# Retention and channel mix on one core: one group of channel products and its relu pass the state products of the next block and their copy

## The chip, the cores and the metric

The kernel runs on one core of one Trainium2 chip. The metric is the time on the device in microseconds (us), as the median of several executions. The core has five engines with an in-order queue each: TensorE (PE in the profile; PEld is its loading of weights), VectorE (DVE), ScalarE (ACT), GpSimd (POOL) and SyncE (SP). TensorE writes its results to PSUM, which has 8 banks of 128 x 512 float32; the kernel names them 0 to 7.

## The reference

Two layers follow each other. The first is a retention layer over 4 batches, 8 heads, 768 tokens and head width 64: a state of 64 x 64 per head that decays by gamma at each token and takes up k times v.

```python
for t in range(S):
    state = gamma[None, :, None, None] * state + np.einsum('bhd,bhe->bhde', k[:, :, t], v[:, :, t])
    y[:, :, t] = scale * np.einsum('bhd,bhde->bhe', q[:, :, t], state)
```

Its output, with the heads side by side (512 columns), is the x of the second, a channel mix with a shift by one token:

```python
xk = mu_k * x + (1.0 - mu_k) * x_prev
xr = mu_r * x + (1.0 - mu_r) * x_prev
k = np.maximum(xk @ w_k, 0.0)          # 512 -> 1024
v = k * k @ w_v                        # 1024 -> 512
r = 1.0 / (1.0 + np.exp(-(xr @ w_r)))
return (r * v).astype(np.float32)
```

## The kernel before, in words

The 768 tokens of each batch are worked off in three blocks of 256, so there are 12 blocks, 0 to 11; block 3 is the first of batch 1. A block goes through these steps, each with a code:

- `lq`, `lk`, `lv` load q, k and v (`load`, lines 222 to 237), most of them issued by GpSimd. `vs` scales v by powers of gamma into float16 (`scale_v`, L253).
- `Tq`, `Tk` transpose q and k on TensorE (L272, L278), `Eq`, `Ek` copy the result out of PSUM. `S` multiplies k by q (L318, L331, L339), `M` masks it on VectorE (L347, L354).
- `C` makes the state products k times v of the block in two halves, one PSUM bank each (`state`, L384 for blocks 2 to 5: 16 matmuls). `U.n.c` adds half c to the state that is carried along (`summed`, L419); in the first block of a batch there is nothing to add to, and `U.n.0` is a plain copy of the first half into float16 (L407 to 417, by way of `copy`, L241). `G` multiplies the state by the decay of 256 tokens for the next block (`decayed`, L424).
- `I` multiplies the carried state by q (L441), `Y` the masked scores by v (L462, L478), `D` scales the sum into x (L507, L514).
- `dx` and `X` make xk and xr (`differ`, `mixed`). `K.n.g` is a group of the channel products xk @ w_k (`keys`, L582 for a block by itself, L572 for two blocks together): for block 2 a group is two slices of 128 of the 1024 channels, eight matmuls, and the four groups fill one bank each. `Qa.n.g` is the relu of a group, from its bank into a buffer (`relued`, L591), `Qb.n.g` the square of that (`squared`, L599, L603), both on ScalarE.
- `R` and `s` are the gate xr @ w_r and its sigmoid (L612, L618), `V` is the product with w_v (L624, L642), `O` the product with the gate (L630, L649), `st` the store (L637, L657).

What sets the order of the work is a text, `ORDER` (lines 24 to 81), written out by hand: one word for a step, `code.block.part`, then `@` and the PSUM banks or `~` and the engine (v VectorE, a ScalarE, p GpSimd, s SyncE). The loop at lines 755 to 769 walks through it and issues each step; with the manual schedule (line 179) each engine gets its instructions in just this order. Waits follow from what is written and read: a step that writes a bank waits until what was in it has been read.

The change touches line 40 of the text. The words before it that matter are on line 39: `K.2.2@5 Qa.2.2~a K.2.3@4` and `Qa.2.3~a Qb.2.3~a`, `S.3.1@67 M.3.1~v`. Line 40 reads:

```python
S.3.0@01 vs.3~p C.3@23 U.3.0~a Qb.2.2~a K.2.1@4 Qa.2.1~a K.2.0@2 Qa.2.0~a I.3@45 lq.6~p vs.4~v
```

and line 41 begins `C.4@67 U.3.1~v X.2.1.1~v V.0.1.0@3 M.3.0~v V.1.0.0@2 G.3~a U.4.0~v I.4@01`. Here `vs.3` is one of the two scalings that GpSimd does. K.2.1 uses bank 4 as K.2.3 before it; C.3 uses banks 2 and 3; K.2.0 uses bank 2 after C.3. `KR` (line 150) is the set of four buffers between `Qa` and `Qb`, given out in the order in which they come free (lines 588 to 597).

Of the kernel before, what the change touches and what calls it, by code (L numbers as in the profile page):

```python
# [36 lines left out]
Qa.1.2~a s.1.0~a X.0.1.2~v X.0.1.1~v X.0.1.0~v R.0.1@5 s.0.1~a s.1.1~a R.0.0@7 s.0.0~a S.4.1@01  # L37
Qb.1.0~a D.2~v dx.2~v X.2.0.2~v X.2.0.0~v S.4.0@23 Tq.3@4 Eq.3~a X.2.0.1~v wv.1~p X.2.0.3~v Tk.3@7
lq.5~p Ek.3~a K.2.2@5 Qa.2.2~a K.2.3@4 M.4.1~v M.4.0~v Qa.2.3~a Qb.2.3~a lk.6~p S.3.1@67 M.3.1~v
S.3.0@01 vs.3~p C.3@23 U.3.0~a Qb.2.2~a K.2.1@4 Qa.2.1~a K.2.0@2 Qa.2.0~a I.3@45 lq.6~p vs.4~v  # L40
C.4@67 U.3.1~v X.2.1.1~v V.0.1.0@3 M.3.0~v V.1.0.0@2 G.3~a U.4.0~v I.4@01 X.2.1.3~v U.4.1~v J.3
Qb.1.3~a Y.4 Qb.2.0~a lk.5~p X.2.1.2~v X.2.1.0~v Y.3 D.3~v dx.3~v V.0.0.0@7 V.0.1.1 O.0.1~v Tq.5@45
J.4 D.4~v dx.4~v R.2.0@6 Qb.2.1~a V.0.0.1 O.0.0~v X.3.0.1~v Eq.5~a Qb.1.2~a V.1.0.1 X.3.0.2~v
# [756 lines left out]
```

## Time and profile before

| | |
|---|---|
| median of 3 runs | 153.38 us (153.35 to 153.46) |
| the profiled execution | 153.28 us |
| its span, first to last instruction | 151.4 us |
| granted TensorE clock, mean | 1.000 |
| busy: DVE, ACT, POOL | 127.8, 103.6, 55.3 us |
| HBM read, written | 24.16 MB, 6.29 MB |

A row of the time line gives start and duration in us, the engine, the line of the kernel, the operation, the tile written and the tiles read, the shapes, and how many instructions are put together in it. In brackets stands how long the engine was idle before it, and what ended that. Matmuls are pipelined: each lasts longer than the distance from its start to the next one's start, so rows of PE overlap. The chain of waits is followed back from the last instruction to what released each step.

### The profile page before, as it was taken

To read this page: it belongs to the slowest core of one execution; us is meant where nothing else is said; L and a number is where in the kernel's file an instruction comes from. 1 tells how busy PE (TensorE), PEld (TensorE's weight loads), DVE (VectorE), ACT (ScalarE), POOL (GpSimd) and SP (SyncE) were. 2 spreads that over 40 slices of the span, in tenths; PEclk is the share of its full clock that TensorE was granted. 3 is DMA by queue.
4 is the path that set the end of the run, shared out by engine and by line. 5 is a ranking of instruction groups with operands and counts; after the bars stand their busy time and mean duration, and the time that the engine had idled before them with its cause. 6 is when DMAs were issued, how large, how long until landed. Compare 5 with 4: busy or idle time off the path is not lost.

```text
span 151.4 us, 5541 instructions
## 1 busy us (share of the span) xinstructions
PE 143.4 (95%) x2426; PEld 82.8 (55%) x2426; DVE 127.8 (84%) x212; ACT 103.6 (68%) x195; POOL 55.3 (37%) x65
## 2 busy tenths in 40 slices
PE   7878799999999999999999999999999999999991
PEld 3345487757754554547465564548456444655450
DVE  7886999999989999999999999999799999400432
ACT  3565979899844795779567786999604756839420
POOL 7953998577957309996710000000000000000000
PEclk9999999999999999999999999999999999999999
DMA  5999999999999999999999019301000005500433
GB/s 140 219 229 197 207 231 192 168 251 212 196 167 202 233 262 107 256 300 198 231 173 126 7 38 283 105 35 45 0 4 0 4 0 211 205 0 0 148 133 139
DMA packets 45624, 22.16 MB, mean 146 GB/s; under 512 B 37400, under 2 KB 41248, under 8 KB 45600
## 3 DMA queue, kind: packets, MB, share of 16 engines
q0 software_dynamic: 38704, 14.42, 74.5%
q1 hardware_dynamic: 6592, 7.21, 14.3%
q8 instruction: 19, 0.31, 0.8%
q10 hardware_dynamic: 304, 0.18, 0.4%
q14 instruction: 5, 0.04, 0.1%
HBM read 24.16 MB, written 6.29 MB: 201 GB/s over the span
## 4 chain that ended last, share of the span: by engine, by line
PE 73%; DMA 12%; POOL 11%; issue 1%; DVE 0%; POOLq 0%
PE ps L624 27%; PE ps L572 14%; DMA v<-in_v_dram 12%; PE ps L612 12%; PE ps L582 8%; PE ps L278 3%; POOL q L235 3%; POOL k L230 2%; PE ps L441 2%; POOL vs L253 2%; POOL v L230 2%; PE ps L366 1%; PE ps L462 1%; PE ps L642 1%; PE ps L318 1%
## 5 line engine op out<-in xcount | busy, mean ns | idle before, releaser
L624 PE MATMUL ps<-wv,k2s 128*128 128x512 f16 x184 | 44.1, 380 | 0.0
L591 ACT ACTIVATE kr<-ps 128x512 f32<-128x512 f32 x48 | 27.9, 594 | 12.5 <-PE ps L582 6.5
L624 PEld LDWEIGHTS <-k2s 128*128 128x128 f16 x184 | 17.1, 98 | 18.9 <-ACT k2s L603 0.4
L630 DVE SCALAR_TENSOR_TENSOR os<-ps,rs 128x512 f32<-128x512 f32 x23 | 15.6, 684 | 11.9 <-ACT rs L618 9.4
L612 PE MATMUL ps<-wr,xr 128*128 128x512 f16 x96 | 23.5, 379 | 0.0
L582 PE MATMUL ps<-xk,wk 128*128 128x256 f16 x192 | 23.2, 273 | 0.0
L572 PE MATMUL ps<-xk,wk 128*128 128x512 f16 x96 | 23.0, 379 | 0.0
L618 ACT ACTIVATE rs<-ps 128x512 f32<-128x512 f32 x24 | 13.6, 597 | 12.9 <-PE ps L612 12.1
L230 POOL DMA_DIRECT2D k<-in_k_dram x20 | 17.8, 903 | 10.3 <-PE ps L384 6.7
L582 PEld LDWEIGHTS <-wk 128*128 128x128 f16 x192 | 18.1, 98 | 3.7
L241 ACT COPY qT<-ps 128x1024 f16<-128x1024 f16 (+1 forms) x13 | 12.3, 946 | 9.5 <-PE ps L278 7.8
L558 DVE SCALAR_TENSOR_TENSOR xr<-dx,mu,xT 128x256 f16<-128x256 f32 (+1 forms) x32 | 17.9, 577 | 0.1
L230 POOL DMA_DIRECT2D v<-in_v_dram x18 | 16.0, 911 | 3.6 <-DMA wr<-in_moe_w_r_dram 1.9
L558 DVE SCALAR_TENSOR_TENSOR xk<-dx,mu,xT 128x256 f16<-128x256 f32 (+1 forms) x32 | 17.0, 579 | 0.2
L354 DVE TENSOR_TENSOR a<-ps,c_sb 128x1024 f16<-128x1024 f32 (+1 forms) x14 | 14.6, 1066 | 0.9 <-PE ps L339 0.6
L603 ACT ACTIVATE k2s<-kr 128x512 f16<-128x512 f32 x24 | 14.8, 631 | 0.3
L612 PEld LDWEIGHTS <-xr 128*128 128x128 f16 x96 | 9.0, 97 | 10.7 <-issue 0.5
L572 PEld LDWEIGHTS <-wk 128*128 128x128 f16 x96 | 9.1, 98 | 10.5
L599 ACT ACTIVATE k2s<-kr 128x512 f16<-128x512 f32 x24 | 14.5, 627 | 0.3
L241 ACT COPY kT<-ps 128x1024 f16<-128x1024 f16 (+1 forms) x13 | 12.2, 945 | 2.2 <-PE ps L272 1.7
L529 DVE TENSOR_TENSOR dx<-xT 128x1024 f32<-128x1024 f32 x11 | 13.4, 1221 | 0.2
L253 DVE TENSOR_TENSOR vs<-v,csm_sb 128x1024 f16<-128x1024 f32 x10 | 12.2, 1217 | 0.2 <-DMA v<-in_v_dram 0.2
(73 smaller groups left out, 165.6 us busy)
## 6 DMA issues: line engine op xcount, KB each, us to landing
out_dram<-os SPq DMA_DIRECT2D x23, 256.0 KB, 2.4
v<-in_v_dram POOLq DMA_DIRECT2D x18, 256.0 KB, 7.7
q<-in_q_dram POOLq DMA_DIRECT2D x11, 256.0 KB, 8.4
k<-in_k_dram POOLq DMA_DIRECT2D x21, 128.0 KB, 8.8
v<-in_v_dram POOLq DMA_DIRECT2D x2, 512.0 KB, 7.2
wk<-in_moe_w_k_dram POOLq DMA_DIRECT2D x2, 512.0 KB, 10.4
wv<-in_moe_w_v_dram POOLq DMA_DIRECT2D x2, 512.0 KB, 10.4
wr<-in_moe_w_r_dram POOLq DMA_DIRECT2D x1, 512.0 KB, 8.7
```

The costliest lines, as they stand in the source:

```text
L230: e.dma_start(out=dst[:, :, i * D : i * D + D], in_=src[:, i * P : i * P + P].rearrange("h p d -> p h d"),)
L241: e.copy(out=out, in_=in_)
L253: e.tensor_tensor(out=VS(n), in0=V32(n).rearrange("p h (i d) -> p i h d", i=2), in1=gks[:, int(half(n) or wide(n)), :, :, None].to_broadca ...
L354: nc.vector.tensor_tensor(out=a_full(n)[:, i, :, j0:j1], in0=pairs(banks("S", n, i, j0))[:, :, j0:j1], in1=(below if wide(n) else causal[: ...
L558: nc.vector.scalar_tensor_tensor(out=XM[w](k)[:, j, t0:t1], in0=DX(k)[:, j, t0:t1], scalar=mu[:, w * NCO + j : w * NCO + j + 1], in1=x[:, ...
L572: nc.tensor.matmul(banks("K", n, g), lhsT=wk16[:, co, g * P : g * P + P], rhs=XM[0](k)[:, co, :], start=(co == 0), stop=(co == NCO - 1),)
L582: nc.tensor.matmul(pz[:, i, :], lhsT=wk16[:, co, fo * P : fo * P + P], rhs=XM[0](k)[:, co, m * TM + t0 : m * TM + t1], start=(i == 0 and c ...
L591: nc.scalar.activation(out=kr, in_=banks("K", n, g, *u), func=AF.Relu)
L603: nc.scalar.activation(out=K2(n)[:, w * g : w * g + w, t0:t1], in_=kr.rearrange("p a t -> p (a t)").rearrange("p (i t) -> p i t", i=w), fu ...
L612: nc.tensor.matmul(banks("R", n, tb), lhsT=XM[1](k)[:, co, t : t + P], rhs=wr16[:, co, :], start=(co == 0), stop=(co == NCO - 1),)
L624: nc.tensor.matmul(banks("V", n, tb), lhsT=K2(n)[:, fo, tb * P : tb * P + P], rhs=wv16[:, fo, :], start=(fo == 0), stop=(fo == NFO - 1),)
L630: nc.vector.scalar_tensor_tensor(out=OS(2 * n + tb), in0=banks("V", n, tb), scalar=1.0 / (KSC * KSC), in1=RS(2 * n + tb), op0=ALU.mult, op ...
```

## The change

Two words of the order, `K.2.1@4` and `Qa.2.1~a`, move from behind `Qb.2.2~a` to the place in front of `C.3@23`. On TensorE the eight matmuls of K.2.1 then come ahead of the sixteen of C.3; on ScalarE the relu Qa.2.1 comes ahead of the copy U.3.0 and of the square Qb.2.2. All else keeps its place. The text gets a line more, so the lines of the kernel behind it are numbered one higher (K is L583, C.3 is L385).

```diff
-S.3.0@01 vs.3~p C.3@23 U.3.0~a Qb.2.2~a K.2.1@4 Qa.2.1~a K.2.0@2 Qa.2.0~a I.3@45 lq.6~p vs.4~v
+S.3.0@01 vs.3~p K.2.1@4 Qa.2.1~a C.3@23 U.3.0~a
+Qb.2.2~a K.2.0@2 Qa.2.0~a I.3@45 lq.6~p vs.4~v
```

## The prediction

> **What bounds the kernel now.** I read the page's busy times first, then the chain of work that ended last, then what TensorE waits for, and last the time line of each engine around the edited line of the order. The page:
>
> ```profile
> PE 143.4 (95%) x2426; PEld 82.8 (55%) x2426; DVE 127.8 (84%) x212; ACT 103.6 (68%) x195; POOL 55.3 (37%) x65
> PE 73%; DMA 12%; POOL 11%; issue 1%; DVE 0%; POOLq 0%
> ```
>
> TensorE (PE) is busy for 95% of the span, and the chain that ends last is 73% PE. The chain in order of time shows where it goes over to PE (start, duration, what):
>
> ```profile
> 25.54 10.37 DMA v<-in_v_dram
> 35.91 0.07 issue
> 35.98 1.91 POOL vs L253
> 37.89 0.04 issue
> 37.93 0.44 PE ps L384 x16
> 38.37 1.85 PE ps L582 x16
> 40.23 0.23 PE ps L441 x4
> ...
> 148.26 0.02 issue
> ```
>
> So up to 37.93 us the end is set by the load of block 3's v and by GpSimd's scaling of it (`vs.3`). From 37.93 to 148.26 it is PE without a break: C.3 (L384) is the first link, and the 16 matmuls behind it are K.2.1 and K.2.0, eight each. PE's waits from 38 us to the end, and its busy time there, say the same:
>
> ```profile
> PE ps L384 <- POOL vs L253: 0.3, 1, 0.3
> 38.00:148.30 110.30, 110.24 (x1816) 1.00 0.74 126
> ```
>
> There is one wait, the one in front of C.3 (it lies just before 38 us; the group that it released reaches into the window), and 110.24 us busy of 110.30, at a granted clock of 1.00. Whatever the edit adds or saves on PE at about 38 us therefore comes out at the end with almost nothing to soak it up. The time line of PE, then of ScalarE (ACT), around the edit:
>
> ```profile
> 35.12 1.92 PE L582 MATMUL ps<-xk,wk 128*128 128x256 f16 x16
> 36.98 0.62 PE L331 MATMUL ps<-qT,kT 64*128 64x128 f16 x16
> 37.93 0.44 PE L384 MATMUL ps<-vs,k 128*64 128x64 f16 x16 [0.33 <-POOL vs L253]
> 38.30 1.92 PE L582 MATMUL ps<-xk,wk 128*128 128x256 f16 x16
> 40.16 0.30 PE L441 MATMUL ps<-qT,tg 64*64 64x128 f16 x4
> ```
>
> ```profile
> 36.60 1.14 ACT L591 ACTIVATE kr<-ps 128x512 f32<-128x512 f32 x2
> 37.77 0.63 ACT L603 ACTIVATE k2s<-kr 128x512 f16<-128x512 f32 x1
> 38.38 0.37 ACT L241 CAST tg<-ps 128x256 f16<-128x256 f32 x1
> 38.65 0.63 ACT L603 ACTIVATE k2s<-kr 128x512 f16<-128x512 f32 x1
> 39.45 0.60 ACT L591 ACTIVATE kr<-ps 128x512 f32<-128x512 f32 x1 [0.17 <-PE ps L582]
> 40.32 0.60 ACT L591 ACTIVATE kr<-ps 128x512 f32<-128x512 f32 x1 [0.28 <-PE ps L582]
> 40.82 1.05 ACT L424 ACTIVATE tg<-t,csm_sb 128x64 f16<-128x64 f32 x4
> ```
>
> PE in words: K.2.2 and K.2.3, S.3.0, 0.33 us idle, C.3, K.2.1 and K.2.0, I.3. ACT: Qa.2.2 and Qa.2.3, Qb.2.3, U.3.0 (the cast), Qb.2.2, Qa.2.1, Qa.2.0, G.3.
>
> **The change part by part.** No instruction is added or dropped, and the built program has the same rows in another order: on PE the eight matmuls of K.2.1 now stand ahead of the sixteen of C.3; on ACT Qa.2.1 stands ahead of U.3.0 and Qb.2.2. The two moved steps issue no DMA and pass no word of GpSimd's or SP's. So the question is only what each step waits for in its new place. Steps on one PSUM bank must follow each other, and the banks stand in the order: K.2.1 is on bank 4, which K.2.3 used before and Qa.2.3 empties; C.3 is on banks 2 and 3; K.2.0 is on bank 2, which U.3.0 empties of C.3's first half.
>
> *1. K.2.1 goes into the idle time: little of it is left to win.* S.3.0 ends at 36.98 + 0.62 = 37.60. But bank 4 is free only when Qa.2.3 ends, the second of the pair 36.60 + 1.14 = 37.74. For the delay from such an end to PE's start I take 0.05 us: the scaling on GpSimd ends at 35.98 + 1.91 = 37.89 in the chain (37.88 in its own row), and C.3 starts at 37.93; an ACT to PE release shows the same:
>
> ```profile
> 7.08 0.59 ACT L241 COPY qT<-ps 128x512 f16<-128x512 f16 x1
> 7.72 0.42 PE L339 MATMUL ps<-qT,kT 64*64 64x128 f16 x16 [0.69 <-ACT qT L241]
> ```
>
> (7.67 to 7.72.) K.2.1 starts at 37.79. The idle time shrinks from 0.33 to 0.19.
>
> *2. C.3 follows K.2.1.* Sixteen matmuls of this form start 0.11 us apart and one takes 0.27 (0.27 + 15 x 0.11 = 1.92), so eight take 1.04: K.2.1 ends at 38.83. A group of small matmuls behind such a group starts 0.06 us ahead of its end (S.3.0 at 36.98 against 35.12 + 1.92 = 37.04; I.3 at 40.16 against 40.22): C.3 runs from 38.77 to 39.21. Its `vs.3` has then been ready since 37.88, its banks too, so the wait of the old order is gone for good, with 0.9 us to spare.
>
> *3. K.2.0 loses its cover.* In the old order K.2.1 stood between C.3 and K.2.0, for 0.88 us (eight starts 0.11 apart, so that K.2.0 started at 39.18), while U.3.0 took 0.37; the copy cost PE nothing. In the new order nothing stands between, and U.3.0 is late as well, since ACT works in order and Qa.2.1 stands before it. Qa.2.1 starts when K.2.1 has ended; the release from PE to ACT is 0.11 us (K.2.1 of the old order ends at 38.30 + 1.04 = 39.34, Qa.2.1 starts at 39.45). So Qa.2.1 runs from 38.94 to 39.54. U.3.0 overlaps its end by up to 0.10 us, as Qb.2.2 does with U.3.0 (38.38 + 0.37 = 38.75 against 38.65) and G.3 with Qa.2.0 (40.92 against 40.82); it starts at 39.44 and ends at 39.81. C.3's bank 2 is ready at 39.2, so the queue on ACT is what decides, by about 0.2 us. With 0.05 of release K.2.0 starts at 39.86, where the old order has it at 39.18. PE is idle from 39.21 to 39.86, 0.65 us, twice what the old gap was.
>
> The Trainium skill, Perfetto Trace Analysis, section Matmuls (under Optimizing Tensor Performance), speaks against this step: independent matmul groups should rotate through different PSUM banks, so that the evacuation of one lies under the matmuls of the next. K.2.0 directly behind C.3 on bank 2 is the opposite; by that rule a wait of at least the copy is due, and the old trace agrees in so far as the 0.37 us cast lay under K.2.1.
>
> *4. The sum.* K.2.0 then takes what it took, 0.98 us to I.3's start (39.18 to 40.16): I.3 starts at 39.86 + 0.98 = 40.84 against 40.16. That is **+0.68 us**. By parts against the old order, in PE's time up to K.2.0's first matmul: with no wait of either kind K.2.1 would start at 37.53 (0.07 ahead of S.3.0's end, as K.2.1 of the old order stands 0.07 ahead of C.3's end), C.3 0.98 later and K.2.0 another 0.37 later (as 37.93 to 38.30 now), at 38.88, that is 0.30 earlier than now; the wait on Qa.2.3 gives 0.26 of it back (-0.04); the wait on U.3.0 adds 0.72 (+0.68).
>
> *5. Behind it.* Who waits for the moved steps? U.3.1 on VectorE (DVE) needs U.3.0, and U.4.0 needs G.3:
>
> ```profile
> 39.76 0.42 DVE L419 TENSOR_TENSOR t<-ps,tg 128x256 f32<-128x256 f32 x1
> 40.49 1.22 DVE L354 TENSOR_TENSOR a<-ps,c_sb 128x1024 f16<-128x1024 f32 x1
> 41.90 0.42 DVE L419 TENSOR_TENSOR tg<-ps,tg 128x256 f16<-128x256 f32 x1 [0.20 <-ACT tg L424]
> 42.59 0.42 PE L441 MATMUL ps<-qT,tg 64*64 64x128 f16 x12
> ```
>
> U.3.1 starts at 39.86 in place of 39.76, 0.10 late, and DVE has 0.20 idle before U.4.0; free. On ACT Qa.2.0 starts 0.11 behind K.2.0's end (39.86 + 1.04 = 40.90), at 41.01, so G.3 ends 0.69 late; U.4.0 shifts by the same and I.4 (42.59, 0.27 behind U.4.0's end) keeps its slack, since PE shifts too. On GpSimd one load of k must wait until C.3 has read its buffer:
>
> ```profile
> 40.50 0.90 POOL L230 DMA_DIRECT2D k<-in_k_dram  x1
> ```
>
> The first issue comes at 40.50, C.3 ends at 39.21: covered by 1.3 us. I cost all of this at nothing. If the cover failed, each of these is a delay on PE of a few tenths, which is the upper end below.
>
> *6. What could be given back.* After 38 us two groups of gate products (L612) start late on a DVE result, without an idle time that the profile shows:
>
> ```profile
> 30.86 2.76 PE L612 MATMUL ps<-wr,xr 128*128 128x512 f16 x12
> ...
> 64.67 1.89 PE L572 MATMUL ps<-xk,wk 128*128 128x512 f16 x8
> 66.55 1.24 PE L612 MATMUL ps<-wr,xr 128*128 128x512 f16 x5
> ...
> 127.19 2.86 PE L612 MATMUL ps<-wr,xr 128*128 128x512 f16 x12
> ```
>
> ```profile
> 65.81 0.68 DVE L630 SCALAR_TENSOR_TENSOR os<-ps,rs 128x512 f32<-128x512 f32 x1
> ```
>
> Twelve such matmuls take 2.76 us at 30.86 and 2.86 at 127.19, 0.10 more. Twelve in 2.76 and eight in 1.89 mean 0.22 apart, so the one at 66.55 could have come at 64.67 + 8 x 0.2165 = 66.40: 0.15 late (its bank 2 is emptied by the result step of the last row, 65.81 + 0.68 = 66.49, and 0.06 of release). If DVE kept its old times there, PE would lose 0.25 less. But DVE itself is shifted at U.4.0 by G.3, and it works in order; I take 0, with 0.25 as the end of the range.
>
> The profiled execution took 153.28 us, its span 151.4. The sum gives 153.96 for it. The median of the three runs is 153.38, 0.10 above; nothing in the sum touches that, so the forecast is 153.38 + 0.68 = **154.06 us**.
>
> **The rivals.**
>
> *Part is given back (13 in 100).* The shift is +0.68 at 40 us and shrinks at 66.55 and 127.19 by up to 0.25, or U.3.0 starts on ACT a little sooner: +0.35 to +0.55, 153.73 to 153.93. For it: those two waits are there. Against it: DVE's queue is held up by the same G.3.
>
> *More is lost (8 in 100).* U.4.0, late by ACT's queue, comes later than I.4 needs it, or the releases take longer than 0.05 and 0.11: +0.85 to +1.1, 154.23 to 154.5. Against it: 0.27 us of slack at I.4, and each release was read off two rows.
>
> *The gap is filled and was a long one (faster, 3 in 100).* In the timed runs the load of v could land later than in the profiled one (35.91), so that the old order stands longer in front of C.3. K.2.1 then covers that time, up to the 0.88 us that it takes, so the edit costs 0.68 less the lateness: it breaks even at a load 0.68 us later, that is 1.0 us of idle time in the old order. Later than that, Qa.2.1 is over before C.3 and no longer holds up the cast; K.2.0 then waits for the cast and two releases alone, 0.04 + 0.37 + 0.05 = 0.46, and the edit gains 0.88 - 0.46 = 0.42: 152.96 us, or 153.0 to 153.2 on the way there. Against it: the runs shown lie within 0.11 us of each other and 0.10 of the profiled one, so a load 0.7 us later is not in them. The Trainium skill, Perfetto Trace Analysis, section Optimization Strategy, points to this side: find the gaps on the most contended engine and make what they wait for come sooner or finish faster. Read so, the edit would be worth the gap, some 0.3 us (an estimate from the 0.33 row); by the rows above the gap is moved, not closed.
>
> *Only the first wait counts (4 in 100).* -0.04 to +0.2, no change: U.3.0 slips ahead of Qa.2.1, or K.2.0 waits for no copy. The built order of ACT speaks against the first, the banks against the second. That the edit doesn't do what it says I leave at nothing, since the built order shows it.
>
> **How the numbers follow.** Forecast +0.68, with its own ends +0.55 and +0.85 (releases and overlaps of 0.05 to 0.1 each): 72 in 100, 153.93 to 154.23. A measurement of this kernel can tell about 0.2%, 0.31 us, from no change. Slower by more than that: 72 + 13 + 8 = 93; within it 4; faster 3. For 8 in 10 the range takes in nearly all of the first rival, below the forecast, and a part of the second, above it: 153.75 to 154.32.
>
> **What would show it.** In the profile after: K.2.1 (eight of line 583) at 37.8 and then C.3 (L385) at 38.8 with no wait for `vs`; on ACT relu, cast, square in place of cast, square, relu; the cast ending at 39.8; PE idle for 0.6 to 0.7 us before the second eight, ended by ACT's `tg`; I.3 at 40.84; and the same shift of 0.68 at the last matmul (148.9). I am wrong if PE's second eight start before 39.6, if the wait in front of K.2.1 is not ended by ACT, or if the shift at 148 us is not that at 41 us.

## The result, and the profile after

The changed kernel takes 154.25 us (median of 6 runs, 154.17 to 154.58) against 153.36 of the kernel before beside it (6 runs, 153.12 to 153.46): a ratio of 1.0065, 95% interval 1.0052 to 1.0078, so 0.8 to 1.2 us slower, 1.0 in the middle. (The ratio goes by the means, 154.31 and 153.30; the two medians lie 0.89 apart.) The forecast was slower by 0.68, that is 154.06, with 153.75 to 154.32 as the range. A ratio of 1.0065 on its 153.38 is 154.38, just above that range; the median of 154.25 by itself lies inside it. Two runs in a slower state, 155.51 and 158.08 us, are in none of the ratios of this document. The profiled execution took 154.19 us with a span of 152.4, 1.0 us longer than the one of before.

The page of the changed kernel, busy time and chain, which answers to the first fence of the prediction:

```profile
PE 143.8 (94%) x2426; PEld 82.9 (54%) x2426; DVE 127.9 (84%) x212; ACT 103.5 (68%) x195; POOL 55.3 (36%) x65
PE 74%; DMA 10%; ACT 5%; POOL 5%; issue 3%; DVE 1%; DVEq 0%; ACTq 0%; POOLq 0%
```

PE's work is the same within 0.4 us; a link of ScalarE (5%) is new in the chain, and GpSimd has lost 6 points. The time line of PE around the edit, and PE's waits from 36 us to the end:

```profile
37.31 0.62 PE L332 MATMUL ps<-qT,kT 64*128 64x128 f16 x16
38.13 1.03 PE L583 MATMUL ps<-xk,wk 128*128 128x256 f16 x8 [0.19 <-ACT kr L592]
39.09 0.44 PE L385 MATMUL ps<-vs,k 128*64 128x64 f16 x16
40.17 1.03 PE L583 MATMUL ps<-xk,wk 128*128 128x256 f16 x8 [0.64 <-ACT tg L242]
41.13 0.30 PE L442 MATMUL ps<-qT,tg 64*64 64x128 f16 x4
```

```profile
PE ps L583 <- ACT tg L242: 0.6, 1, 0.6
PE ps L583 <- ACT kr L592: 0.2, 1, 0.2
```

The wait for `vs` is gone, and the two forecast waits stand in its place with the forecast sizes: 0.19 in front of K.2.1 (0.19 forecast), ended by the relu, and 0.64 in front of K.2.0 (0.65 forecast), ended by the cast. ScalarE in the same stretch shows why the second is as long:

```profile
36.94 1.14 ACT L592 ACTIVATE kr<-ps 128x512 f32<-128x512 f32 x2
38.11 0.63 ACT L604 ACTIVATE k2s<-kr 128x512 f16<-128x512 f32 x1
39.26 0.60 ACT L592 ACTIVATE kr<-ps 128x512 f32<-128x512 f32 x1 [0.52 <-PE ps L583]
39.75 0.37 ACT L242 CAST tg<-ps 128x256 f16<-128x256 f32 x1
40.00 0.64 ACT L604 ACTIVATE k2s<-kr 128x512 f16<-128x512 f32 x1
```

The cast starts 0.11 before the relu's end at 39.86 (39.26 + 0.60), 0.22 after C.3 ended at 39.53: it stood in the queue. So the picture around the edit is the one that was drawn. But every row stands later than drawn, and already the first: S.3.0 (L332) starts at 37.31, where the old profile has it at 36.98, and S.3.0 lies ahead of everything that the change moved. I.3 is 0.97 later than in the old profile: 0.33 of that was there before the edit, 0.64 comes at it. Followed back along the chain of waits, the 0.33 arises at block 2's scaling of v on VectorE, which in this execution waited for its load:

```profile
24.62 1.23 DVE L254 TENSOR_TENSOR vs<-v,csm_sb 128x1024 f16<-128x1024 f32 x1 [0.50 <-DMA v<-in_v_dram]
```

In the old profile the same row starts at 24.27 with no wait. From I.3 on nothing is given back: I.3 is 0.98 late (by the trace's nanoseconds), the last matmul 0.99.

### The profile page after: what moved, and what is told of

It reads as the page before. It is cut to its first block, busy times and chain, and to the rows that moved or that the text cites. A ratio compares the mean times of both kernels' runs of the same rounds, so it can differ in the third digit from the quotient of the medians.

```text
span 152.4 us, 5541 instructions
## 1 busy us (share of the span) xinstructions
PE 143.8 (94%) x2426; PEld 82.9 (54%) x2426; DVE 127.9 (84%) x212; ACT 103.5 (68%) x195; POOL 55.3 (36%) x65
## 4 chain that ended last, share of the span: by engine, by line
PE 74%; DMA 10%; ACT 5%; POOL 5%; issue 3%; DVE 1%; DVEq 0%; ACTq 0%; POOLq 0%
PE ps L625 27%; PE ps L573 14%; PE ps L613 12%; DMA v<-in_v_dram 10%; PE ps L583 10%; PE ps L279 3%; PE ps L442 2%; POOL q L236 2%; ACT rs L619 1%; ACT qT L242 1%; PE ps L367 1%; PE ps L463 1%; ACT kr L592 1%; PE ps L643 1%; PE ps L319 1%
## 5 line engine op out<-in xcount | busy, mean ns | idle before, releaser
L583 PE MATMUL ps<-xk,wk 128*128 128x256 f16 x192 | 23.5, 273 | 1.0 <-ACT tg L242 0.6
L583 PEld LDWEIGHTS <-wk 128*128 128x128 f16 x192 | 18.1, 98 | 5.0 <-issue 0.8
```

The costliest lines, as they stand in the source:

```text
L583: nc.tensor.matmul(pz[:, i, :], lhsT=wk16[:, co, fo * P : fo * P + P], rhs=XM[0](k)[:, co, m * TM + t0 : m * TM + t1], start=(i == 0 and c ...
```

## The experiments

The question was whether the 0.33 us ahead of the edit is the change's own doing (theory B: the new program makes that load land late), or scatter from one execution to the next that the old order hides and the new one does not (theory A): in the old order C.3 starts at the later of two things, the end of `vs.3` on GpSimd and the end of PE's own stage, S.3.0. If the first profile of before had PE's stage early by chance, its 0.33 us of idle time is no property of the old order.

### Both kernels again, for their traces

No edit; two more traces of the kernel before and two more of the changed one.

> The kernel before once more, for its trace alone. Two theories of the 0.3 us that the result has over the forecast. Theory A (lateness passed on): at about 24.3 us the scaling of block 2's v waits for its load, and the load lands later in some executions than in others; the old order hides up to 0.33 us of that under its wait for vs.3. Then here S.3.0 (the 16 matmuls before C.3) may start anywhere from 36.9 to 37.4 us, C.3 starts at 37.9 to 38.0 all the same, the idle time in front of C.3 shrinks by as much as S.3.0 is late, and the time stays at 153.1 to 153.5. Theory B (the new program itself makes that load land later): S.3.0 at 36.98 within 0.05, the idle time 0.33 again, and the load of block 2's v is never waited for at 24.3 us.

> The kernel before a third time, for its trace. Theory A: C.3 starts at the later of the end of vs.3 (37.8 to 38.0) and S.3.0's start plus 0.6; S.3.0 to I.3 takes 2.82 where S.3.0 starts after 37.3 us, more by the difference where it starts sooner. The time is 153.0 to 153.5.

> The changed kernel once more, for its trace alone. Both theories: from the start of S.3.0 to the start of I.3 it takes 3.82 us (3.18 before), with idle times of 0.19 and 0.64. Theory A: the start of S.3.0 moves by some tenths from execution to execution (37.31 in the first profile), and the time moves with it, one for one, 153.85 to 154.6. Theory B: S.3.0 at 37.31 within 0.05 and 154.2.

> The changed kernel a third time, timed against the one before. Theory A: S.3.0 starts anywhere from 36.9 to 37.7, S.3.0 to I.3 takes 3.82 all the same, and the profiled time is S.3.0's start plus 116.9 (37.31 gave 154.19, 37.65 gave 154.52). The old order loses 0.33 at C.3 only in those executions in which vs.3 ends later than PE's stage, so the ratio stands for 0.64 to 1.00 us: 1.0042 to 1.0065, time 154.0 to 154.4. Theory B (the new program makes its load land late each time): S.3.0 at 37.3 to 37.65 again and a ratio of 1.0065.

The kernel before, second trace (153.30 us), PE and GpSimd's `vs.3`:

```profile
37.42 0.62 PE L331 MATMUL ps<-qT,kT 64*128 64x128 f16 x16
38.02 0.44 PE L384 MATMUL ps<-vs,k 128*64 128x64 f16 x16
38.39 1.92 PE L582 MATMUL ps<-xk,wk 128*128 128x256 f16 x16
40.24 0.30 PE L441 MATMUL ps<-qT,tg 64*64 64x128 f16 x4
```

```profile
35.87 1.92 POOL L253 TENSOR_TENSOR vs<-v,csm_sb 128x1024 f16<-128x1024 f32 x1
```

There is no idle time in front of C.3: S.3.0 is 0.44 later than in the first profile and C.3 only 0.09. `vs.3` ended at 37.79, before PE asked for it. The third trace (153.31 us):

```profile
36.93 0.62 PE L331 MATMUL ps<-qT,kT 64*128 64x128 f16 x16
37.53 0.44 PE L384 MATMUL ps<-vs,k 128*64 128x64 f16 x16
37.90 1.92 PE L582 MATMUL ps<-xk,wk 128*128 128x256 f16 x16
39.75 0.30 PE L441 MATMUL ps<-qT,tg 64*64 64x128 f16 x4
```

```profile
35.26 1.92 POOL L253 TENSOR_TENSOR vs<-v,csm_sb 128x1024 f16<-128x1024 f32 x1
```

Here PE's stage is as early as in the first profile, and `vs.3` is early too: it ends at 37.18, not at 37.8 to 38.0 as I expected, so there is again no idle time, where I expected some. C.3 still starts at the later of the two, and both of them scatter. So the wait of 0.33 us, which the edit was to fill and with which my sum began, is in one of three traces of the old order. Without it the old order takes 2.82 us from S.3.0 to I.3; with it, 3.18; 2.94 is the mean of the three.

The changed kernel, third trace (153.91 us in the profiled execution, 154.04 as the median of 10 runs against 153.17, ratio 1.0050, 1.0020 to 1.0080):

```profile
37.03 0.62 PE L332 MATMUL ps<-qT,kT 64*128 64x128 f16 x16
37.84 1.03 PE L583 MATMUL ps<-xk,wk 128*128 128x256 f16 x8 [0.19 <-ACT kr L592]
38.81 0.44 PE L385 MATMUL ps<-vs,k 128*64 128x64 f16 x16
39.88 1.03 PE L583 MATMUL ps<-xk,wk 128*128 128x256 f16 x8 [0.64 <-ACT tg L242]
40.85 0.30 PE L442 MATMUL ps<-qT,tg 64*64 64x128 f16 x4
```

S.3.0 is early in this one (block 2's scaling starts at 24.33 without a wait), and S.3.0 to I.3 takes 3.82 as in the first (37.31 to 41.13) and in the second trace (37.65 to 41.47, 154.52 us). The profiled times, 153.91, 154.19 and 154.52, are S.3.0's start plus 116.88, 116.88 and 116.87: the new order passes on each tenth. Theory B as it was stated falls, since the late load is not in each trace of the new kernel; A stands. A weaker B, that the new program makes the load late more often, is not excluded: over all the experiments but the pair that moves this load, block 2's scaling waits for it in five of the seven traces with K.2.1 ahead of C.3 and in one of the five with the old order. S.3.0 starts at 37.33 and 37.22 us on average there, from 37.03 to 37.65 and from 36.93 to 37.51, so these few traces can't tell such an effect, of about 0.1 us, from scatter. Where the scatter ahead of 37 us comes from is only partly known: it is the load of block 2's v in two of the three traces of the new kernel, while in the second trace of the old one VectorE's masks are already 0.46 late at 11 us (11.33 against 10.87).

### The cast ahead of the relu on ScalarE

```diff
-S.3.0@01 vs.3~p K.2.1@4 Qa.2.1~a C.3@23 U.3.0~a
+S.3.0@01 vs.3~p K.2.1@4 C.3@23 U.3.0~a Qa.2.1~a
```

> The changed kernel, but on ScalarE the cast U.3.0 stays ahead of the relu Qa.2.1 (only TensorE's part of the change is left, and Qa.2.1 is still ahead of Qb.2.2). If the wait in front of K.2.0 is made by ScalarE's queue, as in step 3 of the prediction, the cast starts 0.04 behind C.3's end, and the idle time falls from 0.64 to 0.46; S.3.0 to I.3 takes 3.64 in place of 3.82, and the time is 0.18 less than the changed kernel's. Rival: the wait is the copy with its releases and the queue does not matter: 0.64 and no change.

```profile
37.42 0.62 PE L332 MATMUL ps<-qT,kT 64*128 64x128 f16 x16
38.24 1.03 PE L583 MATMUL ps<-xk,wk 128*128 128x256 f16 x8 [0.19 <-ACT kr L592]
39.20 0.44 PE L385 MATMUL ps<-vs,k 128*64 128x64 f16 x16
40.07 1.03 PE L583 MATMUL ps<-xk,wk 128*128 128x256 f16 x8 [0.43 <-ACT tg L242]
41.04 0.30 PE L442 MATMUL ps<-qT,tg 64*64 64x128 f16 x4
```

The wait in front of K.2.0 falls from 0.64 to 0.43 (0.46 expected), S.3.0 to I.3 to 3.62. So 0.2 of the cost was ScalarE's queue. By the clock the ratio to the kernel before is 1.0053, 1.0034 to 1.0072. The trace shows the difference to the changed kernel; the times alone do not tell it from the 1.0065, and the same holds for the two experiments that follow.

### K.2.1 on an empty bank

```diff
-S.3.0@01 vs.3~p K.2.1@4 Qa.2.1~a C.3@23 U.3.0~a
+S.3.0@01 vs.3~p K.2.1@5 Qa.2.1~a C.3@23 U.3.0~a
```

> The changed kernel with K.2.1 on bank 5 (empty since Qa.2.2) in place of bank 4 (empty after Qa.2.3). By step 1 of the prediction the idle 0.19 in front of K.2.1 goes, K.2.1 starts 0.26 earlier, Qa.2.1, C.3 and the cast with it: S.3.0 to I.3 takes 3.56 in place of 3.82, the time is 0.26 less than the changed kernel's. Rival: the cast is held by something that doesn't move (the wait in front of K.2.0 then grows by what the first one loses): 3.82 and no change.

```profile
37.44 0.62 PE L332 MATMUL ps<-qT,kT 64*128 64x128 f16 x16
37.99 1.05 PE L583 MATMUL ps<-xk,wk 128*128 128x256 f16 x8
38.97 0.44 PE L385 MATMUL ps<-vs,k 128*64 128x64 f16 x16
40.05 1.03 PE L583 MATMUL ps<-xk,wk 128*128 128x256 f16 x8 [0.64 <-ACT tg L242]
41.02 0.30 PE L442 MATMUL ps<-qT,tg 64*64 64x128 f16 x4
```

The first wait is gone, K.2.1 starts 0.55 behind S.3.0's start in place of 0.82, and S.3.0 to I.3 takes 3.58 (3.56 expected); the wait in front of K.2.0 is what it was. Ratio 1.0034, 1.0002 to 1.0067.

### Both together

The two edits above in one kernel.

> The changed kernel with both mendings: the cast U.3.0 ahead of the relu Qa.2.1, and K.2.1 on bank 5. If the two waits are independent, the idle time in front of K.2.1 is gone and the one in front of K.2.0 is 0.43; S.3.0 to I.3 takes 3.82 - 0.26 - 0.20 = 3.36 and the time is 0.45 less than the changed kernel's, about 153.8; 0.5 over the old order's 2.82 with no idle time is left, which is the copy and its releases. Rival (the two waits hide each other): the gain is that of one of them alone, 3.56 to 3.62.

```profile
37.07 0.62 PE L332 MATMUL ps<-qT,kT 64*128 64x128 f16 x16
37.62 1.05 PE L583 MATMUL ps<-xk,wk 128*128 128x256 f16 x8
38.60 0.44 PE L385 MATMUL ps<-vs,k 128*64 128x64 f16 x16
39.48 1.03 PE L583 MATMUL ps<-xk,wk 128*128 128x256 f16 x8 [0.43 <-ACT tg L242]
40.44 0.30 PE L442 MATMUL ps<-qT,tg 64*64 64x128 f16 x4
```

S.3.0 to I.3 takes 3.37 (3.36 expected): the two waits are independent, 0.24 and 0.20. Ratio 1.0043, 1.0023 to 1.0062, 153.66 us against 153.03. What is left over the 2.82 of the old order without idle time is 0.55. Of it 0.51 lies between the starts of C.3 and K.2.0, 0.88 us (38.60 to 39.48) against 0.37 in the old order (38.02 to 38.39 in its second trace): the 0.43 of idle time for the copy and its releases, and the 0.07 or so by which the next group otherwise overlaps C.3's end. The other 0.04 is in the remaining distances, 2.49 against 2.45. That the 0.43 is the open copy is read from the trace, where the cast ends the wait; no run puts K.2.0 on a bank other than C.3's. Neither mend nor both make the new order pay where `vs.3` is in time.

### A `vs.3` that is late, in both orders

The load of block 6's q, 0.9 us of GpSimd, is put ahead of `vs.3`; the same edit in the kernel before and in the changed one.

```diff
-S.3.0@01 vs.3~p C.3@23 U.3.0~a Qb.2.2~a K.2.1@4 Qa.2.1~a K.2.0@2 Qa.2.0~a I.3@45 lq.6~p vs.4~v
+S.3.0@01 lq.6~p vs.3~p C.3@23 U.3.0~a Qb.2.2~a K.2.1@4 Qa.2.1~a K.2.0@2 Qa.2.0~a I.3@45 vs.4~v
```

> The kernel before with one load that GpSimd issues behind vs.3 (block 6's q, 0.94 us) issued ahead of it, so that vs.3 ends 0.94 later, at 38.7 to 39.0; nothing else is moved. Theory A (in the old order C.3 starts at the later of two things, the end of vs.3 and the end of PE's own stage): the idle time in front of C.3 is 0.33 + 0.94 = 1.27 where PE's stage is as early as in the first profile, 0.8 where it is as late as in the second; C.3 starts at 38.8 to 39.0, and the time is 0.8 to 0.95 more, 154.2 to 154.3. Rival (vs.3 is not what held C.3): no change, 153.3.

> The changed kernel with the same load ahead of vs.3. By step 2 of the prediction C.3 starts 0.9 to 1.2 behind the old end of vs.3, so a vs.3 that is 0.94 later is just covered: C.3 at 39.1 to 39.4 without a wait or with one under 0.1, 3.82 to 3.9 from S.3.0 to I.3, 154.25 to 154.4. Against the old order with the same late load it is then within 0.2 us, no longer 1.0 slower: the edit pays only where vs.3 is a microsecond late, as the rival on the faster side had it. Rival to this: the new order also waits for vs.3 and stays 0.6 to 1.0 slower, 155.

The old order with the late scaling:

```profile
37.25 0.62 PE L331 MATMUL ps<-qT,kT 64*128 64x128 f16 x16
38.90 0.44 PE L384 MATMUL ps<-vs,k 128*64 128x64 f16 x16 [1.03 <-POOL vs L253]
39.27 1.92 PE L582 MATMUL ps<-xk,wk 128*128 128x256 f16 x16
41.12 0.30 PE L441 MATMUL ps<-qT,tg 64*64 64x128 f16 x4
```

The new order with it:

```profile
37.41 0.62 PE L332 MATMUL ps<-qT,kT 64*128 64x128 f16 x16
38.22 1.03 PE L583 MATMUL ps<-xk,wk 128*128 128x256 f16 x8 [0.19 <-ACT kr L592]
39.49 0.44 PE L385 MATMUL ps<-vs,k 128*64 128x64 f16 x16 [0.23 <-POOL vs L254]
40.36 1.03 PE L583 MATMUL ps<-xk,wk 128*128 128x256 f16 x8 [0.43 <-ACT tg L242]
41.32 0.30 PE L442 MATMUL ps<-qT,tg 64*64 64x128 f16 x4
```

In the trace of the new order `vs.3` starts 0.6 us later than in that of the old order (36.92):

```profile
37.52 1.92 POOL L254 TENSOR_TENSOR vs<-v,csm_sb 128x1024 f16<-128x1024 f32 x1
```

So `vs.3` ends at 39.44 there (38.84 in the old order), and C.3 waits 0.23 us for it, where under 0.1 was expected. The old order waits 1.03 us in front of C.3 and takes 3.87 us from S.3.0 to I.3; the new one, with the later `vs.3`, takes 3.91, hardly more than its 3.82. The times are the same: 154.16 us (ratio to the kernel before 1.0061, 1.0037 to 1.0085) and 154.17 (1.0060, 1.0039 to 1.0081). The late scaling costs the old order the whole of its lateness and the new one nothing that the clock can tell. The waits of the new order show a second thing: when C.3 is held up past the relu, the relu is out of the way, and the wait in front of K.2.0 falls to 0.43 by itself. So the edit breaks even where the old order would stand idle for about 1.0 us in front of C.3. A cover was bought with it for a case that none of the traces of the kernel before shows: they have 0.33, 0 and 0 us.

### The load of block 2's v earlier, in both orders

This was to take the lateness ahead of the edit away: that load is issued ahead of the load of block 2's q.

```diff
-vs.1~p lq.2~p Tk.1@7
+vs.1~p lv.2~p lq.2~p Tk.1@7
...
-t.0.0.1~a lv.2~p z.2@4
+t.0.0.1~a z.2@4
```

> The changed kernel with the load of block 2's v issued one step earlier on GpSimd, ahead of the load of block 2's q, so that it lands some 0.9 us earlier. Theory A (PE's own stage is late, in part because the scaling of block 2's v at 24.3 us waits 0.26 to 0.54 for this load; the new order passes every tenth of that on): the wait at 24.3 is gone, S.3.0 starts at 37.1 to 37.2 in place of 37.3 to 37.65, S.3.0 to I.3 stays 3.82, and the time falls by 0.2 to 0.4, to 153.9 to 154.1. Rival (the load's lateness is hidden before it reaches S.3.0): S.3.0 and the time stay, 154.25.

> The kernel before with the same one load issued earlier. Theory A: S.3.0 starts at 37.1 to 37.2, but C.3 must wait for vs.3 until 37.8 to 38.0 as ever, so idle time of 0.1 to 0.3 appears in front of C.3 and the time gains at most 0.15 (153.2 to 153.4): the same edit is worth less than half of what it is worth in the new order. Rival (both orders follow PE's stage alike): 0.2 to 0.4 faster, 153.0 to 153.1, with no idle time in front of C.3.

Both expectations were missed: the kernels are slower, 155.97 us (4 runs, ratio 1.0168, 1.0120 to 1.0216) in the new order and 155.74 (4 runs, 1.0138, 1.0073 to 1.0204) in the old. The wait for v is gone, but the load of q is now late, and PE waits for it ahead of block 2's transposes, 0.6 us in the trace of the one and 1.2 in the other. From PE's waits in the old order:

```profile
PE ps L582 <- DVE xk L558: 1.7, 1, 1.7
PE ps L272 <- DMA q<-in_q_dram: 1.2, 1, 1.2
```

So the test doesn't tell A from its rival by the times; the loads stand in one tight row, and what one gains the next loses. In the new order S.3.0 to I.3 is 3.82 once more (37.79 to 41.61), though everything ahead of it differs. The trace of the new order is that of its fastest run, 154.66 us, over 1.2 us below the other three, so what made those as slow is not shown; in the old order's, 155.90 us, the late q and the 1.7 us for `xk` are both in it.

### `vs.3` ahead of a load that isn't urgent

In the kernel before, the load of block 6's k moves behind `vs.3`.

```diff
-lq.5~p Ek.3~a K.2.2@5 Qa.2.2~a K.2.3@4 M.4.1~v M.4.0~v Qa.2.3~a Qb.2.3~a lk.6~p S.3.1@67 M.3.1~v
-S.3.0@01 vs.3~p C.3@23
+lq.5~p Ek.3~a K.2.2@5 Qa.2.2~a K.2.3@4 M.4.1~v M.4.0~v Qa.2.3~a Qb.2.3~a S.3.1@67 M.3.1~v
+S.3.0@01 vs.3~p lk.6~p C.3@23
```

> The old order with the load of block 6's k (two issues on GpSimd, 1.8 us) moved from the place ahead of vs.3 to the one behind it, so that vs.3 starts as soon as its load has landed. Theory A: C.3 is then bound by PE's own stage alone; where that is early the 0.33 us of idle time go, where it is late nothing is won; 0 to 0.3 faster than before, 153.1 to 153.4, and at C.3 no idle time. Rival: vs.3 waits for its load anyway (0.53 us of idle time in the first profile) and starts at 35.9 as ever: no change and the same idle time.

```profile
36.22 1.90 POOL L253 TENSOR_TENSOR vs<-v,csm_sb 128x1024 f16<-128x1024 f32 x1 [2.35 <-DMA v<-in_v_dram]
```

On `vs.3` the rival was right: with nothing ahead of it the scaling waits 2.35 us for its load and starts no sooner than before (36.22). The idle time in front of C.3 is gone all the same, since PE's stage is late in this trace (S.3.0 at 37.51, C.3 at 38.17). Ratio 0.9994, 0.9974 to 1.0014: no difference. None of the orders that were run beats the kernel before.

## Why the prediction was right, and where it was wrong

- **K.2.1 in the idle time (step 1): right.** It waits for Qa.2.3 on bank 4; 0.19 us of idle time forecast, 0.19 seen, 0.24 in S.3.0 to I.3 when another bank takes it away.
- **C.3 free of `vs.3`, with 0.9 us to spare (step 2): right.** It starts 1.78 after S.3.0 (1.79 forecast), 1.0 to 1.3 us after the end of `vs.3` in the three traces, and the late scaling costs the new order nothing that the clock can tell.
- **K.2.0 without cover (step 3): right.** 0.65 of idle time forecast, 0.64 seen in all three traces; the queue's share 0.2 forecast, 0.21 seen; the copy and its releases 0.46 forecast (in the faster rival), 0.43 seen. The rule of the Trainium skill that I set beside it, in Perfetto Trace Analysis, section Matmuls, agrees with the trace: with bank 2 asked for again at once, 0.43 us of copy and releases lay open.
- **Behind it (steps 5 and 6): right.** G.3, U.4.0 and I.4 shifted with PE (each by 0.97 to 0.98 between the first two profiles), and of the two places that could have given something back neither did: 0.98 late at I.3, 0.99 at the last matmul.
- **The sum (step 4): wrong, and this is the step that failed.** It counts the old order's idle time as won, as a term of 0.30 ("at 38.88, that is 0.30 earlier than now"), and starts PE's stage at 36.98. Both come from one profiled execution, and the idle time was in one of three traces of the old order. Without it the term is 0 and the sum by its own other parts is 0.26 + 0.72 = 0.98; the traces give 3.82 - 2.82 = 1.00. With the idle time of the first profile it is 3.82 - 3.18 = 0.64, against 0.68, and as a mean over the three traces of before 0.88. The clock gives 1.00 (0.8 to 1.2) in the first comparison, which leaves 0.68 out, and 0.77 (0.3 to 1.2) in the second, which does not. So that the gap was credited in full is shown; how often it is there in the timed runs is not.
- **The step from the profiled execution to the median: wrong.** "Nothing in the sum touches that" was not true: which of the two things C.3 waits for varies between executions. The old order takes the later of the two, the new one PE's stage in all its three traces. None of the three signs of being wrong that the prediction names came up; none of them puts the gap of the first profile to the test.
- **The rivals.** "More is lost" (+0.85 to +1.1) had the right direction and size, but by luck: neither U.4.0 nor the releases did it. The rival on the faster side had the mechanism that decides, a `vs.3` later than PE's stage, and its break-even at 1.0 us of idle time was met by the pair with the late scaling. I took it only upwards, as a load that could be later than in the profile; it was the profile that had PE's stage early, and the scaling late. The same scatter made the edit dearer.

## What to carry to other kernels

A step put into an idle time is taken from where it stood: look for what it covered there, and price the open evacuation (copy, release and the queue ahead of the copy) against the gap. And an idle time in which one engine waits for another is the difference of two arrival times; where both scatter by as much as the gap, as here (0.5 us for S.3.0, 0.7 for the end of `vs.3` in three traces of one kernel, a gap of 0.33), one trace doesn't give its size. Take a second trace, or give the sum with the gap and without it (here 0.64 and 1.00).

## What the runs showed of the hardware that was not expected

- **Scatter ahead of 37 us.** The twelve traces without the two with block 2's v early have S.3.0 start anywhere from 36.93 to 37.65 us, with the load of block 2's v awaited for 0.26 to 0.58 us in some and not at all in others; the medians of whole batches of the kernel before lie at 153.03 to 153.38.
- **A step of VectorE that took five times as long.** In the old order with block 2's v early, the wait of 1.7 us for `xk` in the fence above is one `xk` step out of four: the four take 3.64 us, where the first profile has 1.67.

```profile
34.64 3.64 DVE L558 SCALAR_TENSOR_TENSOR xk<-dx,mu,xT 128x256 f16<-128x256 f32 x4
36.08 1.91 POOL L253 TENSOR_TENSOR vs<-v,csm_sb 128x1024 f16<-128x1024 f32 x1
```

The last of the four runs from 35.83 to 38.29 and so over the whole of GpSimd's scaling, which in the three traces of the kernel before lies beside VectorE's masking out of PSUM (VectorE's `xk` steps have ended when it starts). With the late scaling in the new order, VectorE's own next scaling of v, which overlaps GpSimd's by 0.38 us, takes 1.47 in place of 1.21. The Trainium skill, Perfetto Trace Analysis, section Optimizing Scalar/DVE Operations, says that GpSimd and VectorE share a read port of SBUF; that this is the cause was not tried, and the trace shows the coincidence alone.

- **A stall of PE with no releaser.** The third trace of the kernel before has 0.52 us of idle time on PE at 58.75, and the trace with `vs.3` first has 0.28 at 59.16, in front of a matmul for which the profile shows nothing that it waited for. In the third trace it eats what the early stage had won (I.3 at 39.75, yet 153.31 us). Its cause stays open.
